# Windowed attention followed by a gated feed-forward layer: the last block's second product by seven products, activation sums four pairs wide, and measured durations in the instruction plan

## The chip, the cores and the metric

The kernel runs on one core of one Trainium2 chip. The metric is the device time of one execution in microseconds (us). The profiler records one execution; the span it shows, first to last instruction, is some 2 us shorter than the time of the same execution (215.9 against 217.69 us in the profiled run of "before").

The engines are called as the profile calls them: PE is TensorE (PEld its weight loads), DVE is VectorE, ACT is ScalarE, POOL is GpSimd, SP is SyncE. A "q" behind a name (SPq, ACTq) is the engine's instruction queue when it issues transfers. L781 is line 781 of the kernel in question; lines shift between kernels, so L781 or L871 of one may be L958 of another.

## The reference

Attention over 4 batches, 8 heads, 768 positions and 64 columns, with a window of 128 and 4 sink positions, followed by a feed-forward layer on 3072 tokens:

```python
def _attn_ref(q, k, v, n_sink, window):
    scores = scale * np.matmul(q, k.transpose(0, 1, 3, 2))
    keep = is_sink | in_window                # 4 sinks, window of 128
    scores = np.where(keep, scores, -1000000000.0)
    a = softmax(scores)                       # written out in the original
    return np.matmul(a, v).astype(np.float32)

def _moe_ref(x, w_in, w_out):                 # 3072 x 512, 512 x 2048, 2048 x 512
    h = x @ w_in
    g = h * (1.0 / (1.0 + np.exp(-1.702 * h)))
    return (g @ w_out).astype(np.float32)
```

What matters here is the last product, `g @ w_out`. Where this document says "second product", it is that one; the first product is `x @ w_in`.

## The kernel before

The kernel works through 12 blocks of 256 tokens. It does not issue instructions as it goes: it describes every operation to a small planner, with the engines that may do it, a duration and a latency in ns for each, what it depends on, and a priority. The planner simulates the engines with those numbers and so fixes the order of every queue. A changed duration in the plan makes no instruction faster; it changes the order.

```python
def cast(n, engs):                            # n columns: (duration, latency) by engine
    ns = {"POOL": (n / 0.96 + 30, n / 0.96 + 130), "DVE": (n / 1.92 + 65, n / 1.92 + 165),
          "ACT": (n / 1.2 + 60, n / 1.2 + 170)}
    return {e: ns[e] for e in engs.split()}
```

In blocks 2 to 10 the second product is done with seven half-size products in place of eight (a Strassen form). It needs sums of activations, `s1`, `s2`, `a11 - a21` and `s4`, made for each block, and four sums of weights, `wf`, made once. The activation sums are made for two pairs of 128-row groups at a time (`w` = 2, operands of 128x256); three of the four go to DVE, one to POOL.

```python
def forms_of_g(k):
    ...
    w = OPT_("GW", 2)
    for s in range(0, NS, w):
        x = slice(s, s + w)
        a11, a21, a12, a22 = (G[:, x, n] for n in range(4))
        s1, s2, s4 = (F[:, x, n] for n in range(3))
        for n, (o_, a, b_, what) in enumerate(((s1, a21, a22, ALU.add), (s2, s1, a11, ALU.subtract),
                                               (a21, a11, a21, ALU.subtract), (s4, a12, s2, ALU.subtract))):
            ...  # one tensor_tensor; n == 2 on POOL, the others on DVE
```

The last block keeps the plain eight-product form. Its second half of rows (`j` = 1) is cut into pieces of 384 and 128 columns, so that the last piece is short. Each piece is scaled out of PSUM and written to memory by two transfers, one for each half of the partitions. The kernel keeps two neighbouring tokens of the output on partitions p and 64 + p, so the row half is a dimension `i` of the output's access pattern:

```python
for j, c0, c1 in ... ((0, 0, 512), (1, 0, 384), (1, 384, 512)):      # last block
    ...  # 16 matmuls of c1 - c0 columns, then a scaling by 0.5 on ACT or DVE
    for i in range(2):
        eng = "ACT" if i and k == NK - 1 and j else "SP"
        def f(...):
            dma.dma_start(
                out[row : row + P, c0:c1].rearrange("(p i) f -> i p f", i=2)[i], O[64 * i : 64 * i + 64, c0:c1])
        o_d = op(eng, 590, (420, 4), f, o_c, prio=prio, kind="out")
```

The softmax here doesn't subtract the row's maximum and nothing guards it: scores larger than these inputs give would overflow.

## Time and profile before

| | before |
|---|---|
| time, median of 4 runs | 218.57 us (218.21 to 218.79) |
| profiled span | 215.9 us |
| PE, DVE, ACT, POOL busy | 97, 80, 68, 45% |
| X, the end of the last matmul of the first product | 204.89 us |
| start of the last matmul of all | X + 7.33 |
| issue of the last transfer | X + 7.91 |
| last packet of data | X + 9.61 |
| end of the span | X + 11.02 |

The lower five rows are read from the records of single instructions and packets. The lines that bound the kernel are shown in the prediction. First, the DMA view over 208 to 218 us, cut in 40 slices of 0.25 us: the busy share of the 16 DMA engines in tenths, and GB/s.

```profile
DMA  9889778410005987920009895401000000000000
GB/s 246 180 197 295 164 205 188 115 16 8 8 33 139 221 213 188 229 58 0 0 25 227 215 309 140 133 0 33 0 0 0 0 0 0 0 0 0 0 0 0
```

Each group of high digits is one output piece, and it is over in about 1.5 us. Second, the transfers to the output by shape (issuing queue, count, KB each, median us from issue to landing):

```profile
out_dram<-osb SPq DMA_DIRECT2D x46, 128.0 KB, 2.4
...
out_dram<-osb SPq DMA_DIRECT2D x1, 32.0 KB, 2.0
out_dram<-osb ACTq DMA_DIRECT2D x1, 32.0 KB, 2.1
```

The last two are the last 128-column piece, one for each half of the partitions.

### The profile page before, as it was taken

The page shows a single profiled execution, that of the slowest core. Times are in us where ns is not written, and L with a number is a line of the kernel's source. Part 1 is how long each engine was busy: PE and PEld are TensorE (multiplying, and loading weights), DVE is VectorE, ACT ScalarE, POOL GpSimd, SP SyncE. Part 2 cuts the span into 40 slices and gives each one's busy share as a digit, 9 for nine tenths or more (in the row PEclk, how much of TensorE's full clock was granted, in tenths as well). Part 3 has the DMA queues.
Part 4 walks back from the last instruction along what each step waited for, and adds up shares of the span by engine and source line. Part 5 has one row for each costly group of instructions (what it writes and reads, how often), then busy time and mean ns, then how long its engine had stood idle before and what let it go on. Part 6 is the DMA issues. An engine that isn't in the chain of part 4 may idle for free.

```text
span 215.9 us, 5898 instructions
## 1 busy us (share of the span) xinstructions
PE 208.8 (97%) x2282; PEld 165.1 (76%) x2282; DVE 172.8 (80%) x410; ACT 146.9 (68%) x289; POOL 97.6 (45%) x155
## 2 busy tenths in 40 slices
PE   7989999999999999999999999999999999999993
PEld 2447777576778877888878888988878988988852
DVE  3677858499998899999898999898898879885520
ACT  2698645799987779669579659679479566535420
POOL 3495446698672682391391393393912112111000
PEclk9999999999999999999999999999999999999999
DMA  5999999999937947928968858989674024024043
GB/s 196 341 235 205 207 304 232 325 300 285 203 58 157 280 95 172 276 52 181 256 102 177 232 131 170 256 175 265 163 146 100 5 49 100 2 54 95 0 98 101
DMA packets 65917, 36.60 MB, mean 170 GB/s; under 512 B 27968, under 2 KB 61120, under 8 KB 65888
## 3 DMA queue, kind: packets, MB, share of 16 engines
q1 hardware_dynamic: 60848, 30.19, 57.8%
q0 software_dynamic: 4592, 5.37, 13.1%
q10 hardware_dynamic: 448, 0.66, 1.0%
q8 instruction: 18, 0.29, 0.6%
q14 instruction: 11, 0.09, 0.1%
HBM read 27.56 MB, written 6.29 MB: 157 GB/s over the span
## 4 chain that ended last, share of the span: by engine, by line
PE 63%; ACT 13%; DVE 12%; DMA 4%; issue 3%; POOL 2%; SPq 0%; DVEq 0%; ACTq 0%; POOLq 0%
PE bank L752 26%; PE bank L871 17%; PE bank L781 6%; ACT at L639 5%; DVE gF L847 5%; PE bank L679 4%; ACT v L295 4%; DVE gT L766 4%; PE bank L614 3%; PE bank L983 3%; ACT th L764 2%; DMA qk<-in_q_dram 2%; POOL qk L295 2%; DMA blkT<-qk 2%; DVE at L646 1%
## 5 line engine op out<-in xcount | busy, mean ns | idle before, releaser
L752 PE MATMUL bank<-xT,w_in 128*128 128x256 f16 x768 | 99.6, 273 | 0.4 <-DVE osb L909 0.3
L764 ACT ACTIVATE th<-bank 128x512 f16<-128x512 f32 x96 | 57.6, 603 | 43.8 <-PE bank L752 42.3
L752 PEld LDWEIGHTS <-w_in 128*128 128x128 f16 x768 | 72.6, 98 | 11.8 <-issue 2.2
L766 DVE SCALAR_TENSOR_TENSOR gT<-th,bank 128x512 f16<-128x512 f16 x96 | 65.3, 681 | 16.4 <-ACT th L764 15.4
L847 POOL TENSOR_TENSOR gT<-gT 128x256 f16<-128x256 f16 x36 | 25.4, 708 | 72.2 <-DVE gF L847 47.7
L639 ACT ACTIVATE at<-bank 128x512 f16<-128x512 f32 (+1 forms) x96 | 49.2, 577 | 6.4 <-PE bank L614 6.3
L295 POOL CAST qk<-qk 64x512 f16<-64x512 f32 (+1 forms) x70 | 43.7, 627 | 6.9 <-DMA qk<-in_q_dram 4.1
L871 PE MATMUL bank<-third,gF 128*128 128x256 f16 x144 | 34.3, 273 | 0.0
L871 PE MATMUL bank<-w_out,gT 128*128 128x256 f16 x144 | 34.1, 273 | 0.0
L871 PEld LDWEIGHTS <-gT 128*128 128x128 f16 x288 | 27.6, 98 | 4.0 <-issue 0.9
L646 DVE TENSOR_TENSOR at<-at,bank 128x1024 f16<-128x1024 f16 (+1 forms) x40 | 25.0, 634 | 4.7 <-ACT at L639 4.7
L295 ACT CAST v<-v 64x512 f16<-64x512 f32 (+1 forms) x42 | 25.4, 604 | 0.8
L781 PE MATMUL bank<-w_out,gT 128*128 128x512 f16 (+2 forms) x112 | 23.7, 349 | 0.0
L871 PEld LDWEIGHTS <-gF 128*128 128x128 f16 x216 | 20.8, 98 | 2.8 <-DVE xb L701 0.3
L679 PE MATMUL bank<-v,at 128*128 128x65 f16 x352 | 21.1, 193 | 1.1 <-DVE at L646 0.7
L679 PEld LDWEIGHTS <-at 128*128 128x128 f16 x352 | 17.3, 97 | 3.3 <-DVE at L646 2.1
L871 PE MATMUL bank<-wf,gT 128*128 128x256 f16 x72 | 17.2, 272 | 0.0
L871 PE MATMUL bank<-w_out,gF 128*128 128x256 f16 x72 | 17.1, 272 | 0.0
L847 DVE TENSOR_TENSOR gF<-gT,gF 128x256 f16<-128x256 f16 x36 | 15.7, 437 | 0.6
L701 DVE TENSOR_TENSOR xb<-bank,rcp 128x256 f16<-128x256 f32 x36 | 15.0, 418 | 0.4
L781 PEld LDWEIGHTS <-gT 128*128 128x128 f16 x112 | 9.9, 98 | 7.0 <-issue 0.3
L679 PE MATMUL bank<-vs,ats 128*128 128x65 f16 x128 | 15.0, 193 | 0.0
(66 smaller groups left out, 208.2 us busy)
## 6 DMA issues: line engine op xcount, KB each, us to landing
out_dram<-osb SPq DMA_DIRECT2D x46, 128.0 KB, 2.4
v<-in_v_dram SPq DMA_DIRECT2D x11, 512.0 KB, 6.4
qk<-in_q_dram SPq DMA_DIRECT2D x8, 512.0 KB, 4.8
qk<-in_k_dram SPq DMA_DIRECT2D x8, 512.0 KB, 5.9
w_in<-in_moe_w_in_dram POOLq DMA_DIRECT2D x4, 512.0 KB, 9.0
w_out<-in_moe_w_out_dram POOLq DMA_DIRECT2D x4, 512.0 KB, 12.4
qk<-in_q_dram SPq DMA_DIRECT2D x6, 256.0 KB, 5.1
qk<-in_k_dram SPq DMA_DIRECT2D x4, 256.0 KB, 4.8
```

The source lines that it names most:

```text
L295: {"POOL": nc.gpsimd.tensor_copy, "DVE": nc.vector.tensor_copy, "ACT": nc.scalar.copy}[e](out=out, in_=in_)
L614: nc.tensor.matmul(f32(o_s, 2 * n + i)[:, c : c + w], src[d, j], Q[d].rearrange("d j s -> d (j s)")[:, q0 : q0 + w], start=k >= KM, stop=T ...
L639: nc.scalar.activation(out=A[:, i, 0:W], in_=f32(o_s, 2 * n + i)[:, 0:W], func=AF.Exp, scale=scale)
L646: nc.vector.tensor_tensor(out=A[:, :, 0:W], in0=A[:, :, 0:W], in1=mask(c0, c0 + W).unsqueeze(1).to_broadcast((P, 2, W)), op=ALU.mult,)
L679: nc.tensor.matmul(avp()[:, j, i], a_, v_, start=(n == 0), stop=(n == len(mms) - 1))
L701: nc.vector.tensor_tensor(out=X, in0=avp()[:, :, :, 0:D], in1=rc.to_broadcast((P, 2, 2, D)), op=ALU.mult)
L752: nc.tensor.matmul(f32(holder[0])[:, bass.ts(e, TB)], w_in16[:, c, bass.ts(Fi, P)], X[:, c] if k < KX else X2[:, :, c], start=(c == 0), st ...
L764: o_t = op("ACT", 477, 600, lambda first=first: nc.scalar.activation(out=th[first.places[0]], in_=f32(first), func=AF.Tanh, scale=0.851), ...
L766: o_g[k, s] = op("DVE", 590, 700, lambda first=first, s=s: nc.vector.scalar_tensor_tensor(out=g[:, 2 * s : 2 * s + 2].rearrange("p a t -> ...
L781: nc.tensor.matmul(f32(holder[0])[:, 0:w], g[:, Fi, bass.ts(j, P)], w_out16[:, Fi, c0:c1], start=(Fi == 0), stop=(Fi == NF - 1),)
L847: (nc.gpsimd if eng == "POOL" else nc.vector).tensor_tensor(out=o_, in0=a, in1=b_, op=what)
L871: nc.tensor.matmul(f32(holder[0])[:, bass.ts(half, N)], lhs, rhs, start=fresh and s == 0 and half == what(0)[0][0], stop=s == NS - 1, skip ...
```

## The change

It has five parts.

1. The last block also goes by seven products. The last product, which two quadrants of the output need, is cut into two pieces of 128 columns so that little is left to do behind the last matmul. The partial sums, outputs and sends are arranged anew in `mm2_last`.
2. In blocks 2 to 10 the activation sums are made four pairs wide (128x512). Their place in the plan's order also moves by one step (`GF`, 5 to 6, not shown in the cut below).
3. The plan gets durations measured on the chip for casts, tanh, the activation product and the sums.
4. The third weight form moves from a shared buffer to one of its own, and block 3's value casts move from ACT to POOL.
5. A fourth PSUM bank may be used for outputs.

The diff, cut to its core:

```diff
-    KS, LASTS = ...'KS',2), ...get('LASTS',NK-1)
+    KS, LASTS = ...'KS',2), ...get('LASTS',NK)
-    wf = [third[...] for n in range(3)]
-    wf += ring("wf", 1, (P, NS, d_model // 2), FP16)
+    wf = [third[...] for n in range(2)]
+    wf += ring("wf", 2, (P, NS, d_model // 2), FP16)
-    plan = Plan(8, {..., "o": OPT_("NO", 3)})
+    plan = Plan(8, {..., "o": OPT_("NO", 4)})
-        ns = {"POOL": (n / 0.96 + 30, n / 0.96 + 130), ...
-              "ACT": (n / 1.2 + 60, n / 1.2 + 170)}
+        ns = {"POOL": (n / 0.96 + OPT_("PC", 100), n / 0.96 + OPT_("PC", 100) + 100), ...
+              "ACT": (n / 1.2 + 100, n / 1.2 + 210)}
-    for k_ in range(KS + 1, NK):
+    for k_ in range(OPT.get("VK", 4), NK):
         CAST_V[k_] = OPT.get("VA", "ACT")
 ...                                    # tanh 477 -> 490, activation product 590 -> 604
-        w = OPT_("GW", 2)
+        w = OPT_("GW", 4) if k < NK - 1 else 2
-   {"POOL": (280 * w, 280 * w + 120), "DVE": (100 * w + 60, 100 * w + 170)}
+   {"POOL": (250 * w + 180, 250 * w + 280), "DVE": (60 * w + 210, 60 * w + 320)}
+    def mm2_last(k):
+        ...
+        m1 = [run(... (G[:, s, 0], W[:, s, 0, 0][:, c : c + V]), h, 0, V, raw, True) for h, c in halves_]
+        ...                             # m2, m4, m5, two halves of m6, m3: as in the other blocks
+        def send(j, c0, w, n, deps, eng):
+            row = k * TB + j * P
+            def f():
+                to = out[row : row + P].rearrange("(p i) f -> i p f", i=2)
+                of = O[:, bass.ts(j, d_model)]
+                if n > 1:
+                    to, of = to.rearrange("i p (n c) -> i p n c", n=2)[:, :, :, c0 : c0 + w], of....[:, :, c0 : c0 + w]
+                else:
+                    to, of = to[:, :, c0 : c0 + w], of[:, c0 : c0 + w]
+                if n == 1:
+                    (nc.scalar if eng == "ACT" else nc.sync).dma_start(to, of)
+                else:
+                    for i in range(2):
+                        (nc.scalar if i else nc.sync).dma_start(to[i], of[64 * i : 64 * i + 64])
+            op(eng, 590, (420, 8), f, deps, prio=nominal(k + 1, 8) + 4, kind="out")
+        send(0, 0, N, 1, [o_11], "SP")
+        send(0, N, N, 1, [o_12], "SP")
+        for (h, c), o6 in zip(halves_, o_6):
+            m7 = run(...)                 # 128 columns
+            o = total(...)                # two quadrants at once, on DVE
+            send(1, c, V, 2, [o], "ACT")
```

So the outputs of the last block leave in two transfers of 128x256 elements with both row halves in one (`n == 1`), and four transfers of one row half each (`n == 2`).

More of the change, by code (lines that the diff above doesn't have):

```diff
@@ L231 @@
     RS, RQ, RV, RA, RX, RG, RTH, RO = 3, 2, 4, 4, 3, globals().get('OPT',{}).get('RG',3), 3, 2
-    KS, LASTS = globals().get('OPT',{}).get('KS',2), globals().get('OPT',{}).get('LASTS',NK-1)
+    KS, LASTS = globals().get('OPT',{}).get('KS',2), globals().get('OPT',{}).get('LASTS',NK)
     pool = ctx.enter_context(tc.tile_pool(name="sb", bufs=1))
@@ L259 @@
     v32.append(third[:, 2 * H * 2 * D :].rearrange("p (h i d) -> p h i d", h=H, i=2))
-    wf = [third[:, 1024 * n : 1024 * n + 1024].bitcast(FP16).rearrange("p (s c) -> p s c", s=NS) for n in range(3)]
-    wf += ring("wf", 1, (P, NS, d_model // 2), FP16)
+    wf = [third[:, 1024 * n : 1024 * n + 1024].bitcast(FP16).rearrange("p (s c) -> p s c", s=NS) for n in range(2)]
+    wf += ring("wf", 2, (P, NS, d_model // 2), FP16)
     gF = ring("gF", 2, (P, NS, 3, P), FP16)
@@ L277 @@
     OPT_ = globals().get("OPT", {}).get
-    plan = Plan(8, {"m": 1, "s": 5, "t": 4, "a": 2, "x": 2, "h": RTH, "o": OPT_("NO", 3)})
+    plan = Plan(8, {"m": 1, "s": 5, "t": 4, "a": 2, "x": 2, "h": RTH, "o": OPT_("NO", 4)})
     op = plan.op
@@ L288, in cast @@
     def cast(n, engs):
-        ns = {"POOL": (n / 0.96 + 30, n / 0.96 + 130), "DVE": (n / 1.92 + 65, n / 1.92 + 165),
-              "ACT": (n / 1.2 + 60, n / 1.2 + 170)}
+        ns = {"POOL": (n / 0.96 + OPT_("PC", 100), n / 0.96 + OPT_("PC", 100) + 100), "DVE": (n / 1.92 + 65, n / 1.92 + 165),
+              "ACT": (n / 1.2 + 100, n / 1.2 + 210)}
         return {e: ns[e] for e in engs.split()}
@@ L763, in mm1 @@
             first, second = holder
-            o_t = op("ACT", 477, 600, lambda first=first: nc.scalar.activation(
+            o_t = op("ACT", 490, 610, lambda first=first: nc.scalar.activation(
                 out=th[first.places[0]], in_=f32(first), func=AF.Tanh, scale=0.851), [second], prio=prio + 2, kind="tanh")
-            o_g[k, s] = op("DVE", 590, 700, lambda first=first, s=s: nc.vector.scalar_tensor_tensor(
+            o_g[k, s] = op("DVE", 604, 710, lambda first=first, s=s: nc.vector.scalar_tensor_tensor(
                 out=g[:, 2 * s : 2 * s + 2].rearrange("p a t -> p (a t)"), in0=th[first.places[0]], scalar=1.0, in1=f32(first),
@@ L817, in forms_of_w @@
         W = w_out16.rearrange("p (s e) (h c) -> p s e h c", e=2, h=2)
-        free_qk, free_v = [o for (kk, _, _), o in o_cqk.items() if kk == 2], [o for p in range(NP) for o in o_cv[2, p]]
+        free_qk = [o for (kk, _, _), o in o_cqk.items() if kk == 2]
         for j in range(4):
@@ L829, in forms_of_w @@
                     deps.append(o_wf[j, 1])
-                o_wf[j, n] = plan.any({"POOL": (1110, 1250), "DVE": (450, 550)}, f, deps + (free_qk, free_qk, free_v, [])[n],
-                                      prio=nominal(KS + 1, OPT_("WFP", -9) + j), kind="wf")
+                o_wf[j, n] = plan.any({"POOL": (1110, 1250), "DVE": (450, 550)}, f, deps + (free_qk, free_qk, [], [])[n],
+                                      prio=nominal(KS + 1, OPT_("WFP", -9) + j) + (OPT_("T3", 0.0) if n == 2 else 0), kind="wf")
     def forms_of_g(k):
@@ L847, in f @@
                     (nc.gpsimd if eng == "POOL" else nc.vector).tensor_tensor(out=o_, in0=a, in1=b_, op=what)
-                o = plan.any({e: {"POOL": (280 * w, 280 * w + 120), "DVE": (OPT_("GD", 100) * w + 60, OPT_("GD", 100) * w + 170)}[e] for e in (OPT_("GE3", "POOL") if n == 2 else "DVE").split()},
-                             f, last if n != 3 else [four[1]], prio=nominal(k, s + OPT_("GF", 5)) + 3, kind="gf")
+                o = plan.any({e: {"POOL": (250 * w + 180, 250 * w + 280), "DVE": (60 * w + 210, 60 * w + 320)}[e] for e in (OPT_("GE3", "POOL") if n == 2 else "DVE").split()},
+                             f, last if n != 3 else [four[1]], prio=nominal(k, s + OPT_("GF", 6)) + 3, kind="gf")
                 last = [o]
@@ L853, in forms_of_g, with at, run, f @@
                 o_f[k, i] = four
+    def mm2_last(k):
+        g, F, O, Z = gT[k % RG], gF[k % 2], osb[k % RO], part
+        G = g.rearrange("p (s e) (t q) -> p s (e t) q", e=2, t=2)
+        W = w_out16.rearrange("p (s e) (h c) -> p s e h c", e=2, h=2)
+        N, V = d_model // 2, d_model // 4
+        u = [0]
+        def at():
+            return nominal(k + 1, 8 * u[0] / 28) + 3
+        def run(what, holder, at_, w, deps, fresh):
+            prev = None
+            for s0 in range(0, NS, 2):
+                def f(s0=s0):
+                    for s in (s0, s0 + 1):
+                        lhs, rhs = what(s)
+                        nc.tensor.matmul(f32(holder[0])[:, at_ : at_ + w], lhs, rhs, start=fresh and s == 0, stop=s == NS - 1,
+                                         skip_group_check=True)
+                o = op("PE", 2 * pe_ns(w), pe_ns(w) + w / 2.4 + 166, f, deps((s0, s0 + 1)) + ([prev] if prev else []), prio=at(),
+                       acq=None if holder else ("o", 1), kind="mm2")
+                u[0] += 0.5
+                if not holder:
+                    holder.append(o)
+                uses("gT", k % RG, o)
+                uses("gF", k % 2, o)
+                prev = o
+            return prev
+        def raw(S):
+            return [o_g[k, s] for s in S]
+        def fw(n, S):
+            return [o_wf[s // 2, n] for s in S]
+        def fg(n, S):
+            return [o_f[k, s][n] for s in S]
+        def read(z, w, src, deps):
+            return op("ACT", w / 1.2 + 50, w / 1.2 + 175, lambda: nc.scalar.mul(Z[:, z : z + w], src(), 0.5), deps, prio=at(), kind="y")
+        def total(dst, src, z, deps, rel):
+            return op("DVE", 335, 440, lambda: nc.vector.scalar_tensor_tensor(
+                out=dst, in0=src(), scalar=0.5, in1=z, op0=ALU.mult, op1=ALU.add), deps, prio=at(), rel=rel, kind="oc")
+        war = reuse("osb", (k % RO, 0)) + reuse("osb", (k % RO, 1)) + reuse("part", 0)
+        ha, hb, h5, hq = [], [], [], []
+        halves_ = ((ha, 0), (hb, V))
+        m1 = [run(lambda s, c=c: (G[:, s, 0], W[:, s, 0, 0][:, c : c + V]), h, 0, V, raw, True) for h, c in halves_]
+        o_1 = [read(3 * N + c, V, lambda h=h: f32(h[0])[:, 0:V], [m] + war) for m, (h, c) in zip(m1, halves_)]
+        run(lambda s: (G[:, s, 2], W[:, s, 1, 0]), hq, 0, N, raw, True)
+        m4 = run(lambda s: (G[:, s, 3], wf[3][:, s]), hq, N, N, lambda S: raw(S) + fw(3, S), False)
+        o_4 = read(N, N, lambda: f32(hq[0])[:, N : 2 * N], [m4] + war)
+        o_11 = total(O[:, 0:N], lambda: f32(hq[0])[:, 0:N], Z[:, 3 * N : 4 * N], [m4, *o_1, o_4] + war, [(hq[0], 0)])
+        m5 = run(lambda s: (F[:, s, 0], wf[0][:, s]), h5, 0, N, lambda S: fg(0, S) + fw(0, S), True)
+        o_5 = read(2 * N, N, lambda: f32(h5[0])[:, 0:N], [m5] + war)
+        m6 = [run(lambda s, c=c: (F[:, s, 1], wf[1][:, s, c : c + V]), h, 0, V, lambda S, o=o: [o] + fg(1, S) + fw(1, S), False)
+              for o, (h, c) in zip(o_1, halves_)]
+        o_6 = [read(c, V, lambda h=h: f32(h[0])[:, 0:V], [m] + war) for m, (h, c) in zip(m6, halves_)]
+        m3 = run(lambda s: (F[:, s, 2], W[:, s, 1, 1]), h5, 0, N, lambda S: [o_5] + fg(3, S), False)
+        o_12 = total(O[:, N : 2 * N], lambda: f32(h5[0])[:, 0:N], Z[:, 0:N], [m3, *o_6] + war, [(h5[0], 0)])
+        def send(j, c0, w, n, deps, eng):
[4 more added lines that the diff above has]
+                if n > 1:
+                    to, of = to.rearrange("i p (n c) -> i p n c", n=2)[:, :, :, c0 : c0 + w], of.rearrange("p (n c) -> p n c", n=2)[:, :, c0 : c0 + w]
+                else:
[9 more added lines that the diff above has]
+        for (h, c), o6 in zip(halves_, o_6):
+            m7 = run(lambda s, c=c: (G[:, s, 1], wf[2][:, s, c : c + V]), h, 0, V, lambda S, o6=o6: [o6] + fg(2, S) + fw(2, S), False)
+            o = total(O[:, 2 * N :].rearrange("p (n c) -> p n c", n=2)[:, :, c : c + V],
+                      lambda h=h: f32(h[0])[:, 0:V].unsqueeze(1).to_broadcast((P, 2, V)),
+                      Z[:, N : 3 * N].rearrange("p (n c) -> p n c", n=2)[:, :, c : c + V], [m7, o_4, o_5] + war, [(h[0], 0)])
+            send(1, c, V, 2, [o], "ACT")
@@ L926, in second @@
     def second(k):
-        if KS <= k < LASTS:
+        if k == NK - 1 < LASTS:
+            mm2_last(k)
+        elif KS <= k < LASTS:
             mm2_by_seven(k)
```

## The prediction

The forecast's sum: 0.35 + 1.7 - 0.2 = 1.85 us, written as about 1.9 and rounded up to 2.1, so 218.6 - 2.1 = 216.5 us. What the profile of "before" shows: matmuls of the two products start 56 ns apart at 128 columns, 109 at 256, 162.5 at 384 and 216 at 512 (medians of the records after 24 us), which the prediction's columns / 2.4 + 2.5 ns meets within 0.3 ns. An activation sum of 128x256 takes 344 to 437 ns on DVE and 708 on POOL, a weight sum of 128x512 on DVE 416 to 585. The last pieces of 32 KB land 2.0 and 2.1 us after issue.

> **What bounds the kernel now.** I read the page first, then the stretches, the groups by shape, the waits, the chain and the timeline of the end. The profiled span is 215.9 us, the median time 218.6 us: some 2.7 us lie outside the span, and I take them as unchanged.
>
> Page, the engines' shares:
>
> ```profile
> PE 208.8 (97%) x2282; PEld 165.1 (76%) x2282; DVE 172.8 (80%) x410; ACT 146.9 (68%) x289; POOL 97.6 (45%) x155
> ```
>
> PE is the bound. But 97% is a mean over overlapping marks: matmuls that start 0.109 us apart are each marked 0.273 us, so a gap under about 0.16 us does not show. I therefore took the start times of all matmuls from the trace and subtracted columns / 2.4 + 2.5 ns from each distance. What remains after the warm-up matmuls is some 12 us. About 6 us of it is regular: 92 to 96 ns at each of the 56 changes between score matmuls on half the rows and full ones, and 0.1 us behind each sink score group. Some 4.8 us are true waits: 1.75 us between 12 and 18 us (the longest 0.855 us, a score bank waiting for an exponential), 3.0 us after 24 us. Most of the latter lie in 72 to 108 us, some in 150 to 160. The stretches (columns: stretch, length, busy us of PE, PEld, DVE, ACT, POOL with counts, clock, DMA share, GB/s) show it coarsely:
>
> ```profile
> 60.00:72.00 12.00, 12.00 (x136) 9.39 (x134) 10.69 (x24) 8.93 (x17) 6.07 (x9) 1.00 0.64 136
> 72.00:84.00 12.00, 11.29 (x140) 9.73 (x139) 11.38 (x27) 10.11 (x21) 8.20 (x13) 1.00 0.79 181
> 84.00:96.00 12.00, 11.81 (x144) 9.94 (x141) 11.36 (x27) 7.99 (x17) 6.13 (x11) 1.00 0.66 170
> 96.00:108.00 12.00, 11.78 (x128) 9.86 (x126) 11.05 (x30) 9.08 (x19) 3.75 (x6) 1.00 0.84 198
> ```
>
> Where PE loses time, DVE is busy 92 to 95%. The waits of that stretch name it:
>
> ```profile
> PEld L679 <- DVE at L646: 1.5, 4, 0.5
> PE bank L679 <- DVE at L646: 0.4, 2, 0.2
> ```
>
> The attention products wait for the mask product, which stands in DVE's queue behind other work. So DVE is a second bound in the middle, and not elsewhere. The end, from the timeline:
>
> ```profile
> 204.02 1.04 PE L752 MATMUL bank<-xT,w_in 128*128 128x256 f16 x8
> 205.33 7.11 PE L781 MATMUL bank<-w_out,gT 128*128 128x512 f16 x48
> 205.53 0.69 DVE L909 SCALAR_TENSOR_TENSOR osb<-bank,part 128x512 f32<-128x512 f32 x1 [0.80 <-PE bank L871]
> 206.14 0.68 DVE L766 SCALAR_TENSOR_TENSOR gT<-th,bank 128x512 f16<-128x512 f16 x1
> 212.10 1.39 ACTq L809 DMA_DIRECT2D out_dram<-osb  x2
> 212.47 0.29 DVE L800 TENSOR_SCALAR osb<-bank 128x128 f32<-128x128 f32 x1 [5.66 <-PE bank L781]
> ```
>
> The last block's second product runs without a gap from 205.33 to about 212.3; then one DVE scaling, an issue at 212.8, packets until about 214.5, and the closing until 215.9.
>
> [...]
>
> **The change part by part.**
>
> (1) The last block by seven products. Removed: 16 matmuls each of 512, 384 and 128 columns, 16384 columns; 16 x 216 + 16 x 162.5 + 16 x 56 ns = 6.95 us (the chain has 6.96). Added: three products in two halves of 128 (48 x 56 ns) and four of 256 (32 x 109 ns) = 6.18 us. PE saves 0.77 us, all on the path, if nothing stalls.
>
> Does anything stall? Let X be the end of the last first-product matmul (before: 204.89). The instruction order of the changed kernel puts behind X, as before, four products of block 10 (to X + 0.44), then all parts on activation pairs 0 to 5 that need no sums (to X + 2.2), only then those on pair 6, 7. In the trace the last activation is ready at 206.82, X + 1.93, because DVE first takes block 10's output sum. So there is 0.27 us in hand. The sums of the last pair then need 0.34, 0.44 and 0.36 us on DVE, ready at about X + 2.3, 2.7 and 3.1; the products on them start at X + 3.1, 4.0 and 4.9. The fourth sum on POOL (0.71 us) must first let the readers of its buffer finish, X + 3.9, used at X + 5.7. The partial sums that ACT reads between (0.38 us for 256 columns) have half a microsecond or more each. I see no stall; PE ends at X + 6.6 instead of X + 7.4.
>
> The finish eats part of it. The last DVE operation grows from 128 to 256 outputs: 0.42 us (row of the 128x256 multiply from PSUM, 418 ns) instead of 0.29. Each 128-column piece now goes out for two row halves in two transfers with 128 runs of 512 bytes each, twice as many as before, and four such transfers plus two larger ones are issued within 1.3 us from two queues at 0.5 to 0.6 us each (issues in the trace stand 0.6 us apart). I put the last issue at X + 7.6 instead of X + 7.9 and the last landing at X + 9.3 to 9.6 instead of 9.6. Net gain of the end: 0.35 us, estimated, between 0 and 0.6.
>
> (2) Activation sums four pairs wide in blocks 2 to 10. The rows:
>
> ```profile
> L847 POOL TENSOR_TENSOR gT<-gT 128x256 f16<-128x256 f16 x36 | 25.4, 708 | 72.2 <-DVE gF L847 47.7 <-PE bank L871 12.1 <-PE bank L752 8.4
> L847 DVE TENSOR_TENSOR gF<-gT,gF 128x256 f16<-128x256 f16 x36 | 15.7, 437 | 0.6
> L847 DVE TENSOR_TENSOR gF<-gF,gT 128x256 f16<-128x256 f16 x36 | 12.9, 359 | 0.9
> L847 DVE TENSOR_TENSOR gF<-gT 128x256 f16<-128x256 f16 x36 | 12.4, 344 | 0.5
> L826 DVE TENSOR_TENSOR third<-w_out 128x512 f16<-128x512 f16 x3 | 1.8, 585 | 0.0
> L826 DVE TENSOR_TENSOR third<-w_out,third 128x512 f16<-128x512 f16 x4 | 1.5, 416 | 0.0
> ```
>
> Before, a block has 4 x (437 + 359 + 344) ns = 4.56 us of sums on DVE. After, it has 2 x 3 instructions of 128x512; the weight sums of that shape take 416 to 585 ns, mean 0.49: 2.9 us. So 1.6 us less DVE per block, 15 us over nine blocks, of which the last block's own sums (12 x 0.38) give 4.6 back at a place where DVE is half idle. In the middle a block takes about 16 us, so DVE falls from 93% to about 83%. That is worth nothing by itself, only as far as PE waited: up to 3.0 us. POOL saves too (2 x 1.15, the row of POOL's weight sum of 128x512, for 4 x 0.71), and is at 45% anyway.
>
> (3) Measured durations in the plan. The plan fixes the order of every queue. Its casts were too short: 487 ns on ACT and 563 on POOL for 512 columns against 619 and 625 in the rows; it now says 527 and 633. Tanh, activation product and sums move likewise. No instruction is made faster; queues stand nearer to the order in which work becomes ready. The order comparison shows most of PE's order changed, from the first scores on.
>
> (4) The third weight form leaves the shared buffer, so it need not wait for block 2's values, and block 3's four value casts move from ACT to POOL: 2.5 us less on ACT about 46 to 50 us; ACT is 95% busy from 48 to 60 us (11.40 of 12), POOL 70%. (5) A fourth output bank is allowed; the end uses it.
>
> Of the 3.0 us of true waits after 24 us I give (2), (3) and (4) together 1.7 us, somewhat more than half: DVE is relieved just where they lie, but dependencies through transposing transfers (4.3 us in the chain at 78 us) stay. The start I leave at zero: the new order puts other matmuls into the 0.855 us wait, but ACT gets one more copy there. Two more row-mode changes (58 for 56) cost 0.2 us. Sum: 0.35 + 1.7 - 0.2 = about 1.9 us; rounded up a little for a start that may gain: 218.6 - 2.1 = 216.5 us.
>
> **The rivals.** (A) The end alone: DVE idles little but PE was waiting for something else, such as ACT or the transposing transfers. For it: ACT also is at 84% in 72 to 84 us, and POOL's casts there waited for late loads. Then 218.2 us. (B) The wide sums come later: each waits for four activation pairs, POOL then works 1.2 us in one piece, and PE waits for sums at each block's start. Against it: the order starts them half a slot later and has other products ready. Time 218.5 to 220. (C) All true waits go, the start's too: 4.8 + 0.35 us, 213.5 us. For it: the new plan is closer to the chip throughout. Against it: the start hangs on loads from memory and on ACT's queue, and the change relieves neither. (D) The end stalls: the four short transfers queue, or the last sums are late; 0.5 us lost, the middle still gained: 217.
>
> **Range and chances.** The middle gives 0.5 to 3 us, the end 0 to 0.6, the start minus 0.5 to plus 1. I take 215.0 to 217.8. Two per cent is 4.4 us, 214.2: that needs nearly all of (C), 0.05. Slower by 2% needs a new stall of 5 us: 0.01.
>
> **What would show it.** Right: the DVE sums of 128x512 near 0.49 us, DVE total near 164 us; PE near full in the stretches from 72 to 108 us and the mask waits gone; 80 second-product matmuls in the end without idle time, in 6.2 us. Wrong: the waits of PE stay the same size with DVE below 85% (A); weight loads of block products waiting for the sums (B); the last transfer landing later behind PE's end than 2.2 us (D).

## More of the kernel before

SP's own waits; L1030 is the end of the program, where SP waits for all outstanding transfers (us in total, times, longest):

```profile
SPq L1030 <- DMA out_dram<-osb: 1.2, 2, 0.9
```

## The result

| | before | after |
|---|---|---|
| time, median of 4 runs each | 218.57 us | 221.27 us (220.95 to 221.43) |
| profiled span | 215.9 us | 218.8 us |
| X | 204.89 | 204.43 |
| start of the last matmul | X + 7.33 | X + 6.55 |
| issue of the last transfer | X + 7.91 | X + 7.82 |
| last packet of data | X + 9.61 | X + 12.74 |
| end of the span | X + 11.02 | X + 14.42 |

The ratio is 1.0123, with a 95% interval of 1.0104 to 1.0143. Ratios here are the mean time of one kernel's fast runs over the mean of the other's in the same rounds, so they are not quite the ratio of the medians. Executions over 1.5% slower than the fastest of the same kernel are left out of the means. The change made the kernel about 2.7 us slower. That is within 2%, as predicted, but on the other side of "before", and outside the range of 215.0 to 217.8 us.

The table says where the time came from before any theory does. At X the changed kernel is 0.46 us ahead; at its last matmul it is 1.24 us ahead; at its last packet it is 2.7 us behind. The head start at X is the least certain of these numbers: six kernels of this document have the same order of work up to X (the changed one, e1, e5, e6, e9 and e10), and their profiles reach it between 203.74 and 204.48 us; the order of "before" reached it at 204.89 here and at 205.62 in e2. The page of the changed kernel has PE busy for less time than before, with more matmuls:

```profile
PE 207.5 (95%) x2314; PEld 167.3 (76%) x2314; DVE 171.1 (78%) x369; ACT 146.2 (67%) x292; POOL 100.4 (46%) x144
```

The middle went roughly as intended. The stretches (columns as in the prediction) and the waits of 60 to 110 us:

```profile
60.00:72.00 12.00, 11.58 (x128) 8.69 (x126) 9.24 (x19) 9.72 (x19) 4.76 (x7) 1.00 0.79 185
72.00:84.00 12.00, 11.77 (x144) 10.29 (x142) 10.58 (x19) 9.21 (x20) 7.18 (x10) 1.00 0.46 109
84.00:96.00 12.00, 12.00 (x147) 10.29 (x146) 10.81 (x24) 7.92 (x17) 5.61 (x9) 1.00 1.01 203
96.00:108.00 12.00, 11.74 (x130) 10.30 (x129) 10.75 (x24) 9.91 (x20) 8.95 (x13) 1.00 0.94 210
```

```profile
PEld L679 <- DVE at L646: 0.5, 1, 0.5
...
PE bank L679 <- DVE at L646: 0.3, 1, 0.3
```

PE gains in 72 to 96 us and loses 0.4 us in 60 to 72 (12.00 to 11.58). DVE has some room, and the weight loads' waits for the mask product fell from 1.5 us (four waits) to 0.5 us (one). The same account of matmul starts that gave 3.03 us of true waits after 24 us gives 1.60 us now. The groups of the sums, by shape:

```profile
L847 POOL TENSOR_TENSOR gT<-gT 128x512 f16<-128x512 f16 x18 | 22.1, 1228 | 63.9 <-DVE gF L847 61.8 <-PE bank L679 1.9
...
L847 DVE TENSOR_TENSOR gF<-gT,gF 128x512 f16<-128x512 f16 x18 | 11.5, 641 | 0.3
L847 DVE TENSOR_TENSOR gF<-gF,gT 128x512 f16<-128x512 f16 x18 | 10.7, 592 | 0.3
L847 DVE TENSOR_TENSOR gF<-gT 128x512 f16<-128x512 f16 x18 | 7.6, 421 | 0.3
```

The end, from the timeline:

```profile
204.86 1.49 PE L873 MATMUL bank<-w_out,gT 128*128 128x128 f16 x18
...
209.02 2.38 SPq L927 DMA_DIRECT2D out_dram<-osb  x2
...
210.14 1.06 PE L873 MATMUL bank<-wf,gT 128*128 128x128 f16 x16
210.41 1.25 DVE L898 SCALAR_TENSOR_TENSOR osb<-bank,part 128x256 f32<-128x256 f32 x3 [1.87 <-PE bank L873]
211.25 1.44 ACTq L930 DMA_DIRECT2D out_dram<-osb  x2
211.50 1.38 SPq L930 DMA_DIRECT2D out_dram<-osb  x2
```

The products run without a visible gap, DVE is done at 211.66, and the last issue stands at 212.25. No engine computes anything after that, yet the span lasts to 218.85. The chain of waits does not show why: it ends with the DVE operation at 211.24. The DMA view over 208 to 218 us can (0.25 us a slice, as before):

```profile
DMA  8892006961111120111111358975961111110000
GB/s 197 188 221 49 16 25 156 213 160 25 33 49 49 37 33 12 20 45 49 45 45 51 74 102 215 219 133 121 258 180 45 51 45 47 43 41 25 0 0 0
```

Read the runs of 1. A tenth and a bit is 2 engines of 16 (0.125), and 41 to 51 GB/s is what moves meanwhile. From 210.25 us until 213.5 (with a dip at 211.75), and again from 215.5 until 217.25, the strip shows about two engines at work and the rest idle. The burst of high digits in between is the four short transfers, beside the second joined one. Taking the packets one by one: there are 256 packets of 1 KB, those of the two `n == 1` transfers. They run from 210.24 to 216.73 us with 2.02 in flight on average. The last 512-byte packet, of the short transfers, ends at 217.17. The transfers by shape and SP's closing wait say the same:

```profile
out_dram<-osb ACTq DMA_DIRECT2D x2, 64.0 KB, 5.2
out_dram<-osb SPq DMA_DIRECT2D x2, 64.0 KB, 5.7
```

```profile
SPq L1119 <- DMA out_dram<-osb: 4.2, 3, 3.0
```

The four short transfers, issued last, land after 5.2 and 5.7 us, where the last piece before took 2.0. The two long ones are hidden in the group of 46 transfers of 128 KB.

### The profile page after: what moved, and what is told of

Same layout as the page of the kernel before. It is cut to its first block, busy times and chain, and to the rows that moved or that the text cites. A ratio compares the mean times of both kernels' runs of the same rounds, so it can differ in the third digit from the quotient of the medians.

```text
span 218.8 us, 5877 instructions
## 1 busy us (share of the span) xinstructions
PE 207.5 (95%) x2314; PEld 167.3 (76%) x2314; DVE 171.1 (78%) x369; ACT 146.2 (67%) x292; POOL 100.4 (46%) x144
## 4 chain that ended last, share of the span: by engine, by line
PE 79%; DVE 9%; ACT 6%; issue 2%; ACTq 0%; DVEq 0%
PE bank L752 34%; PE bank L958 20%; PE bank L679 6%; PE bank L781 6%; PE bank L614 4%; PE bank L1072 3%; ACT at L639 3%; PE bank L873 3%; DVE gF L847 3%; DVE gT L766 2%; ACT v L295 2%; PE bank L542 1%; DVE xb L701 1%; DVE at L646 1%; ACT th L764 1%
## 5 line engine op out<-in xcount | busy, mean ns | idle before, releaser
L847 POOL TENSOR_TENSOR gT<-gT 128x512 f16<-128x512 f16 (+1 forms) x22 | 24.9, 1133 | 73.4 <-DVE gF L847 66.5
L295 POOL CAST qk<-qk 64x512 f16<-64x512 f32 (+1 forms) x70 | 44.9, 644 | 13.0 <-DMA qk<-in_q_dram 10.4
L958 PE MATMUL bank<-third,gF 128*128 128x256 f16 x144 | 34.1, 273 | 0.0
L958 PEld LDWEIGHTS <-gT 128*128 128x128 f16 x288 | 27.5, 98 | 4.1 <-issue 0.9
L958 PE MATMUL bank<-wf,gT 128*128 128x256 f16 x144 | 27.0, 272 | 0.0
L295 ACT CAST v<-v 64x512 f16<-64x512 f32 (+1 forms) x38 | 22.9, 603 | 0.8
L781 PE MATMUL bank<-w_out,gT 128*128 128x512 f16 x64 | 15.9, 379 | 0.0
L614 PEld LDWEIGHTS <-blkT 64*128 64x128 f16 x256 | 8.0, 94 | 8.4 <-issue 6.6
L847 DVE TENSOR_TENSOR gF<-gT,gF 128x512 f16<-128x512 f16 (+1 forms) x22 | 13.4, 608 | 0.3
```

The source lines that it names most:

```text
L295: {"POOL": nc.gpsimd.tensor_copy, "DVE": nc.vector.tensor_copy, "ACT": nc.scalar.copy}[e](out=out, in_=in_)
L614: nc.tensor.matmul(f32(o_s, 2 * n + i)[:, c : c + w], src[d, j], Q[d].rearrange("d j s -> d (j s)")[:, q0 : q0 + w], start=k >= KM, stop=T ...
L781: nc.tensor.matmul(f32(holder[0])[:, 0:w], g[:, Fi, bass.ts(j, P)], w_out16[:, Fi, c0:c1], start=(Fi == 0), stop=(Fi == NF - 1),)
L847: (nc.gpsimd if eng == "POOL" else nc.vector).tensor_tensor(out=o_, in0=a, in1=b_, op=what)
L958: nc.tensor.matmul(f32(holder[0])[:, bass.ts(half, N)], lhs, rhs, start=fresh and s == 0 and half == what(0)[0][0], stop=s == NS - 1, skip ...
```

## The experiments

T1 says: the two joined transfers run on about two DMA engines of the sixteen (2.02 packets in flight over both). Their packets then take 6.5 us, and the short transfers queue behind them. What sets these two apart is that the row half, a dimension of size 2, stands outermost in them, where the kernel before picks one half by `[i]`. That this is the cause was an inference at this point; e1 and e2 test it, by splitting and by joining. That both joined transfers went by the same two engines is an inference as well; the records of the changed kernel agree with it: each of the four short transfers has 16 landing events, of which 14 come within 0.2 to 0.8 us of each other (the last of them at 215.24 to 215.84 us) and the other two 1.1 to 2.0 us later (216.34 to 217.61). In "before" the 16 of each of the last two pieces of 32 KB come within 0.21 and 0.31 us.

The rivals: the new end as a whole is slow (its many issues and short packets, or its last sums), or the loss comes from the middle and shows only at the end. Later runs ask why the gain stays smaller than predicted once T1's cost is taken away, and what the other parts of the change are worth. Eleven kernels ran, in three sets, each set on one chip with its own runs of "before" (medians 218.28, 218.48 and 218.18 us). All ratios are to "before" of the same set.

### e1: the joined transfers split by row half

```diff
                 if n == 1:
-                    (nc.scalar if eng == "ACT" else nc.sync).dma_start(to, of)
+                    for i in range(2):
+                        (nc.scalar if i and c0 else nc.sync).dma_start(to[i], of[64 * i : 64 * i + 64])
```

> The changed kernel, with one edit: the two output transfers of the last block that carry both row halves in one (2 x 64 runs of 1 KB) are issued as two transfers of 64 runs each, one per row half, as the kernel before does everywhere. Theory T1 (these two transfers run on about two DMA engines, 2.0 packets in flight on average, and hold back the last pieces): the 256 packets of 1 KB land within about 1 us of their start instead of 6.5, the last landing moves from 217.2 to about 214.3 us of the span, and the time falls by 2.6 to 3.2 us, to 218.1 to 218.7. Rival T2 (the four pieces of 512-byte runs are what is slow, twice as many runs as before): the time stays above 220.5. Rival T3 (the lost time lies in the new order before the end): nothing changes either.

Measured: 217.70 us (217.39 to 218.11, 6 runs), ratio 0.9975 (0.9958 to 0.9991), somewhat below the 218.1 to 218.7 that T1 expected, and far from T2 and T3. The DMA view over 208 to 218 us, the transfers by shape, and SP's closing wait:

```profile
DMA  9797860018136000783694782000000000010100
GB/s 262 188 221 189 197 139 8 25 49 221 41 106 156 0 0 16 197 230 88 180 252 113 207 228 64 0 0 0 0 0 0 0 0 0 0 33 0 33 0 0
```

```profile
out_dram<-osb SPq DMA_DIRECT2D x5, 64.0 KB, 2.0
out_dram<-osb ACTq DMA_DIRECT2D x3, 64.0 KB, 2.2
```

```profile
SPq L1120 <- DMA out_dram<-osb: 1.7, 1, 1.7
```

The runs of 1 are gone, every piece is a burst of about a microsecond, and the last data lands at 214.18 us, X + 9.76, instead of X + 12.74. Everything else in the kernel is the same. The two joined transfers cost 1.0123 less 0.9975 (each against "before" of its own set), about 1.5% or 3.2 us. T1 holds.

### e2: the kernel before, with one joined transfer

The reverse: nothing of the change but the last block's 384-column piece sent as one transfer.

```diff
+                if k == NK - 1 and c1 == 384 and i:
+                    continue
                 def f(...):
+                    if k == NK - 1 and c1 == 384:
+                        nc.sync.dma_start(out[row : row + P, c0:c1].rearrange("(p i) f -> i p f", i=2), O[:, c0:c1])
+                        return
```

> The kernel before, with one edit: the 384-column piece of the last block goes out in one transfer with the row half as its outermost dimension (2 x 64 runs of 1.5 KB) instead of two transfers. T1: 128 packets at 38 ns (1 KB packets of such a transfer came every 25.6 ns, scaled by size) take about 4.9 us instead of 0.9, and the last pieces of 128 columns wait behind on the shared engines: 3 to 4 us slower than the kernel before, 221.6 to 222.6. T2 and T3: within 0.5 us of the kernel before, as no piece becomes smaller and no order changes.

Measured: 222.48 us (222.09 to 224.62, 4 runs), ratio 1.0212 (1.0174 to 1.0251). The transfers by shape:

```profile
out_dram<-osb SPq DMA_DIRECT2D x1, 192.0 KB
...
out_dram<-osb ACTq DMA_DIRECT2D x1, 32.0 KB, 5.5
out_dram<-osb SPq DMA_DIRECT2D x1, 32.0 KB, 6.0
```

The last, untouched 32 KB transfers now land after 5.5 and 6.0 us instead of 2.1 and 2.0. The joined piece's 128 packets of 1.5 KB took 4.93 us with 2.02 in flight; before, the same packets took 0.88 us with 12.6 in flight. Both cases give the same rate for the pair: 192 KB in 4.93 us is 40 GB/s, 256 KB in 6.49 us is 40 GB/s. One joined transfer in the old kernel brings such a loss without any other part of the change, so the seven-product end and the middle are not needed to explain it.

### e3: the change with the old end

```diff
+OPT = {'LASTS': 11}
```

The last block is done by eight products and sent as in the kernel before; all else is as after.

> The changed kernel with the last block's second product by eight products and its old output pieces; wide sums, measured durations, buffers and cast placement stay. T1: the new order reaches the end 0.46 us earlier than before (204.43 against 204.89 us in the span), so the time is 0.3 to 0.8 us below the kernel before, 217.8 to 218.3. T3 (order or sums lose the time): above 219.5.

Measured: 217.57 us (217.38 to 217.82, 6 runs), ratio 0.9969 (0.9952 to 0.9985). So the other parts of the change are worth 0.3%, about 0.7 us. Compared with e1 in the same set (0.9975), the seven-product end, freed of its joined transfers, shows no gain. That was not expected: its matmuls are 0.77 us shorter. The records of both, counted from X:

| | e3, old end | e1, new end | e6 |
|---|---|---|---|
| start of the last matmul | 7.32 | 6.55 | 6.55 |
| end of the last DVE operation | 7.87 | 7.23 | 7.23 |
| last issue | 7.90 | 7.92 | 7.62 |
| last packet of data | 9.60 | 9.76 | 9.87 |
| end of the span | 11.03 | 11.75 | 11.65 |

PE and DVE keep the gain up to 7.23, and the issue gives it back: SP and ACT are each still busy issuing, at 0.5 to 0.75 us per transfer, and the last issue comes 0.7 us after its data is ready. The closing then takes longer: 1.99 us from the last packet to the end, against 1.43. There SP checks the transfers' semaphores one after another, about 62 ns apart (59 to 69 in "before" and the changed kernel, where a check does not wait), in the same order in both of these. In e1 the one that comes last is second in that order, and nine steps of SP follow it, 0.56 us; in e3 three follow, 0.20 us. That is 0.36 us of the difference. A closing step of GpSimd that takes 0.37 us in e1 (0.38 in the changed kernel) and 0.08 in e3 (and in "before") adds 0.29 us; I did not find its cause. (The first check behind the last packet passed 0.08 us sooner in e1.)

### e4: e1 with sums two pairs wide

```diff
+OPT = {'GW': 2}
```

> As e1, with sums two pairs wide again in all blocks (DVE 1.6 us a block more), planned with the new durations. If the relief of DVE gave the gain in the middle: DVE back to 92 to 95% between 72 and 108 us, waits of the attention products for the mask product back, 0.5 to 1.5 us slower than e1. If the measured durations in the plan alone gave it: within 0.3 us of e1.

Measured: 218.41 us (218.16 to 218.71, 6 runs), ratio 1.0008 (0.9992 to 1.0023): 0.7 us slower than e1 of the same set. True waits of PE after 24 us rose from 2.04 to 2.61 us; DVE was busy 11.39 of 12 us in 96 to 108 us instead of 10.74. The waits of weight loads for the mask product came back only in part (0.7 us in 60 to 110 us, against 0.5 in e1 and 1.5 before). In this plan the width is worth 0.3%.

### e6: the end's issues on a third queue

Split as in e1, and the second quadrant's two transfers issued by GpSimd, so that SP and ACT are free for the last four.

```diff
                     for i in range(2):
-                        (nc.scalar if i and c0 else nc.sync).dma_start(to[i], of[64 * i : 64 * i + 64])
+                        (nc.gpsimd if c0 else nc.sync).dma_start(to[i], of[64 * i : 64 * i + 64])
```

> As e1, with one edit: the two transfers of the quadrant that is ready just before the last two pieces are issued by the idle GpSimd queue instead of one each by the SP and ACT queues. In e1 the last DVE operation ended at 211.65 us and the last issue began only at 212.34, as both queues were still issuing (0.6 to 0.74 us each). T4: last issue 0.3 to 0.5 us earlier, time 0.2 to 0.5 us below e1. T5: within 0.2 us of e1, or slower if a transfer issued from GpSimd lands last.

Measured: 217.83 us (217.27 to 218.24, 6 runs), ratio 0.9961 (0.9936 to 0.9987). The timeline of the end:

```profile
210.45 1.17 POOL L928 DMA_DIRECT2D out_dram<-osb  x2 [3.60 <-DVE osb L898]
210.56 1.37 SPq L931 DMA_DIRECT2D out_dram<-osb  x2
210.56 1.58 ACTq L931 DMA_DIRECT2D out_dram<-osb  x2
```

The last issue came earlier, X + 7.62, but the last packet did not (X + 9.87), as the third column above shows. Issuing is not what holds the end alone: with the queues freed, the data still lands about 9.8 us after X. The interval covers e1, so no gain is shown.

### e5: the product of one quadrant last

e6, and the product that only one quadrant needs (m3) cut in halves of 128 columns, the second half last of all, so that the last transfers are one 128-column quadrant.

```diff
-        o_12 = total(O[:, N : 2 * N], ..., [m3, *o_6] + war, [(h5[0], 0)])
+        o_12 = third_product(0, [])               # 128 columns: products and their sum
 ...
-        send(0, N, N, 1, [o_12], "SP")
+        send(0, N, V, 1, [o_12], "SP")
 ...                                              # the pairs' product and its sends
+        send(0, N + V, V, 1, [third_product(V, [(h5[0], 0)], [o_12])], "SP")
```

> As e6 (below), and the order of the last products changed: the product that only one quadrant of the output needs is cut in two 128-column halves, and its second half is the last product of all, behind the two halves that two quadrants need. The last DVE operation then has 128 outputs instead of 256 (0.29 for 0.42 us), the last piece has 64 runs of 512 bytes in each transfer instead of 128, and the larger pieces leave 0.45 us earlier. Theory T4 (with the two-engine transfers gone, the issues of the last transfers bound the end): 0.3 to 0.8 us faster than e1, 216.9 to 217.4. Rival T5 (the end is bound by PE and the closing alone): within 0.2 us of e1.

Measured: 217.44 us (217.17 to 218.21, 6 runs), ratio 0.9951 (0.9925 to 0.9978). DVE ends at X + 7.19 and the last issue is at X + 8.07, as the queues are busy again with more transfers; the last packet is at X + 9.66. The time is at the upper edge of what T4 expected (216.9 to 217.4). It is the lowest ratio of all, but its interval covers e1, e3 and e6.

### e7: e1 planned with the old durations

```diff
+OPT = {'PC': 30}
-              "ACT": (n / 1.2 + 100, n / 1.2 + 210)}
+              "ACT": (n / 1.2 + 60, n / 1.2 + 170)}
 ...                                    # tanh, activation product and sums as in the kernel before
```

> As e1, but planned with the durations of the kernel before (casts 487 and 563 ns, tanh 477, activation product 590, sums 0.1 us a pair + 0.06 on DVE). Sums stay four pairs wide. If the width of the sums alone gave the gain of the middle (narrow sums cost 0.71 us): within 0.3 us of e1. If the measured durations carry part of it: 0.4 to 1.2 us slower than e1, with more waits of PE after 24 us than the 1.9 us of e1.

Measured: 220.58 us over 6 runs, of which one, the profiled one, was slow (223.94); the five fast runs are 220.35 to 221.24. Ratio of fast runs 1.0090 (1.0062 to 1.0119), some 2.5 us slower than e1. A loss of 0.4 to 1.2 us was expected; it is twice that or more. Its profile does show what the slow run lost: the granted clock was at half from 14.8 to 21.7 us of the span, and half of 6.8 us is 3.4 us, about what this run lies above the others (median of the five: 220.42).

### e8: e1 with block 3's value casts back on ACT

```diff
+OPT = {'VK': 3}
```

> As e1, with the four value casts of block 3 back on ACT. The prediction counted their move as part of the gain: if so, ACT is again 95% busy from 48 to 60 us and the time is 0.2 to 0.8 us above e1. If the move is worth nothing: within 0.2 us.

Measured: 220.08 us (220.01 to 220.87, 6 runs), ratio 1.0078 (1.0049 to 1.0107), some 2.2 us slower than e1. From the stretches, and from the timeline:

```profile
48.00:60.00 12.00, 11.87 (x130) 8.23 (x127) 9.63 (x24) 11.79 (x24) 7.11 (x13) 1.00 0.93 243
```

```profile
81.75 0.29 PE L595 MATMUL bank<-blkT,ks 128*32 128x256 f16 x4 [2.23 <-ACT at L640]
```

ACT is full from 48 to 60 us (11.79 of 12; 10.55 in e1), and at 81.75 us PE stands 2.23 us for a score bank that ACT has not emptied. True waits after 24 us are 4.16 us against 2.04. That one wait is as large as the whole difference. That the early fullness leads to the late wait was not traced step by step.

### e9: half the data in the last transfers

e6, with the four transfers of the last two pieces sending one of their two column blocks only.

```diff
-                        (nc.scalar if i else nc.sync).dma_start(to[i], of[64 * i : 64 * i + 64])
+                        (nc.scalar if i else nc.sync).dma_start(to[i][:, 0:1], of[64 * i : 64 * i + 64, 0:1])
```

> As e6, wrong on purpose: each of the four transfers of the last two pieces sends only one of its two output columns blocks (64 runs of 512 bytes instead of 128), so half of that quadrant pair is never written. Number and place of the issues stay. In e6 the last issue came 0.3 us earlier behind the last first-product matmul than in e1, but the last data did not (9.87 against 9.76 us). Theory T6 (the bytes that are left at the end bound it: 256 KB took 1.44 us in e1): the last data comes 0.5 to 0.8 us earlier, behind the last first-product matmul at 9.1 to 9.4 us, time 0.5 to 0.8 us below e6. T4 (the issues bound it): within 0.2 us of e6.

Measured: 217.49 us (217.23 to 217.67, 5 runs), ratio 0.9968 (0.9955 to 0.9980), the output wrong as intended. The last packet came at X + 9.28, 0.6 us before that of e6, but the closing behind it took 2.13 us instead of 1.78: the span ended at X + 11.42, 0.24 us before that of e6, and the ratio is not lower than that of e6 (0.9961). The last packet came where T6 expected it (9.1 to 9.4), but the 0.5 to 0.8 us of time that T6 expected with it did not come. So the bytes of the last pieces alone are not what sets the time.

### e10: the pairs' product before the single one

```diff
-        m3 = run(...)                    # and its sum and send, moved behind the pairs' product
```

> As e1, with the order of the last products changed: the product that two quadrants of the output need (256 KB of output, in its two halves) before the one that only one quadrant needs (128 KB, in one piece of 256 columns, 64 runs of 1 KB in each of two transfers). All PE work stays. T6: the last data at 9.0 to 9.4 us behind the last first-product matmul instead of 9.76, and 0.3 to 0.7 us faster than e1, ratio to the kernel before 0.994 to 0.996. If the end is bound by PE and a fixed latency alone: within 0.2 us of e1, as PE ends at the same time. If the exchange makes PE wait for the partial sums that ACT reads: slower.

Measured: 217.76 us (217.32 to 218.15, 6 runs), ratio 0.9982 (0.9967 to 0.9996), no better than e1. The last data came at X + 9.74, not at 9.0 to 9.4 as T6 expected: the order of the last two products does not matter here.

### e11: the kernel before with wide sums only

```diff
+OPT = {'GW': 4}
```

> The kernel before with one setting changed: sums four pairs wide, nothing else (old durations, old end, casts of block 3 on ACT). If the relief of DVE (1.6 us a block) is worth something by itself: 0.4 to 1.0 us faster than the kernel before, with fewer waits of PE between 72 and 108 us. If it pays only in a plan whose durations and cast placement fit (undoing either of these cost 2 us): unchanged or slower than before.

Measured: 218.07 us (217.84 to 218.63, 6 runs), ratio 1.0000 (0.9985 to 1.0015). In the old plan the width is worth nothing, though DVE is relieved: PE still waits 2.77 us after 24 us (3.03 before).

### What the set shows together

Without the joined transfers the change is 0.25% faster than before (e1), and the best arrangements of the end measured (e5, e6, e3) are 0.3 to 0.5% faster. They beat both kernels, and I cannot tell them apart from each other. The parts do not add up: the old durations alone cost 2.5 us, block 3's casts alone 2.2 us, the width 0.7 us, and yet the kernel before, which has all three undone together, is only about half a microsecond slower than e1. Each plan is one joint schedule. Taking a part out of one that was tuned with it tells what that plan loses, not what the part is worth. The own buffer of the third weight form (part 4) and the fourth output bank (part 5) were not tried alone.

What bounds the end now stays open. e6 moved the last issue, e9 the last packet as well, and neither moved the time clear of noise; a shorter closing was not tried.

## Why the prediction was right or wrong

**What bounds the kernel: right.** PE is the bound and the true waits lie where the prediction put them. One reading is off: the "2.7 us outside the span" set the median of 218.6 against the span of a faster run; the same execution, of 217.69 us, gives 1.8.

**The step that failed: the finish of part (1)**, "I put the last issue at X + 7.6 instead of X + 7.9 and the last landing at X + 9.3 to 9.6 instead of 9.6." The last landing was X + 12.74. The prediction saw "two larger ones" among the transfers and counted their issues. It did not ask how many engines carry each. The missing term: 256 KB on two engines (2.02 packets in flight). With the 40 GB/s that e2 and the changed kernel show for a pair, that is 6.5 us of packets, from about 1.2 us after the first of the two issues (209.02), so to 216.7; the short transfers queued behind end at 217.2. e1 and e2 show it from both sides: 3.2 us gone when the transfers are split, 4.2 us (medians 222.48 and 218.28) added to the old kernel by joining one.

The hint was in hand: the diff shows `dma_start(to, of)` without the `[i]`. The prediction did not ask what that does to a transfer; e1 and e2 show it. Rival (D), "The end stalls: the four short transfers queue", named the right place and the right symptom, and its test ("the last transfer landing later behind PE's end than 2.2 us") is what came out. But it was sized at 0.5 us with no cause behind it.

**PE of the end: right.** Predicted 0.77 us less, no stall, the last matmul near X + 6.6; measured X + 6.55 against 7.33, and the last DVE operation 0.42 us. **The net gain of the end, 0.35 us: wrong even without the joined transfers.** The last issue of e1 is at X + 7.92, not 7.6, because the queues are still issuing; and the closing, taken as fixed, is 0.56 us longer. e1 against e3 shows no gain.

**Part (2), the sums: the direction right, the size off.** The wide sums take 0.55 us on average (421, 592 and 641 ns), not 0.49. A block saves 4.56 - 3.31 = 1.25 us, not 1.6. DVE's total is 171.1 us, not 164. The sums fell by 6.9 us (41.0 to 34.1), but weight sums on DVE rose by 1.8, and the new end's four 128x256 operations added 1.3. The row that I scaled from, 416 to 585 ns, was of seven instructions in a stretch with other neighbours.

The records of single instructions show what the averages mix. Of the 65 sums of 128x512 on DVE in the changed kernel (54 of activations, 11 of weights), 46 took 0.40 to 0.43 us. The other 19 took 0.47 to 1.37 us; each of them began while POOL was in the middle of a sum or cast, and ended 0.27 to 0.29 us after an instruction of POOL's. In "before", 77 of the 108 sums of 128x256 took 0.26 to 0.29 us, and each of the other 31 (0.62 us on average) began while POOL was at work. So a sum that does not begin beside POOL's work costs 0.285 us at two pairs and 0.42 us at four, and the width by itself saves 12 x 0.285 - 6 x 0.42 = 0.90 us a block. The other 0.35 us come from less time beside POOL: 10.3 us over all of these sums before, 7.0 us after. This reaches PE: the sum at 66.06 us took 1.26 us beside POOL's fourth sum, the mask product behind it in DVE's queue began at 67.24, and at 67.97 PE had stood 0.5 us for it, its longest wait after 24 us. No run took POOL's sums away, so what this costs in time is not shown.

**The middle: the waits nearly right, their worth in time about half.** Waits after 24 us fell by 1.43 us in the changed kernel and by about 1 us in e1, for 1.7 predicted; the waits for the mask product shrank as described. The start, set at zero, lost 0.24 us (1.74 to 1.98). e3 shows what all this is worth in time: 0.7 us, where 1.7 - 0.2 = 1.5 us was predicted for these parts.

**Rivals (A), (B) and (C): not seen.** PE did gain where DVE was relieved, weight loads waited 0.2 us for sums in 60 to 110 us, and not all waits went. (A) has some truth in e11, where relief of DVE alone gives nothing.

**The range** was drawn from the middle and the small terms of the end. No term in it could reach 3 us, so the result could only fall outside.

## What to carry to other kernels

When a diff touches a transfer, read the outermost dimension of both its access patterns before counting issues and bytes. Here, merging two half transfers into one with a dimension of 2 outermost took the packets in flight from 12.6 to 2.02, and the same 192 KB from 0.88 to 4.93 us (e2). Look at the DMA strip over the last 10 us of a profile; a run of ones while the engines do nothing was here a transfer on two DMA engines (2.02 packets in flight told so), and the chain of waits on the engines did not show it: it ended with the DVE operation that begins at 211.24 us of a span of 218.85. And ask of a gain on PE at the very end whether the issue queues and the closing behind it move too. Here they did not: in e1 the last matmul starts 0.77 us earlier than in e3, but the last issue is at X + 7.92 against 7.90, and the closing takes 1.99 us against 1.43.
